# Sigmoid attention and an MLP mixer in one kernel: c1's first half loaded by unit, more dummy products at the start, opening cycles dealt anew, and two stores and two sums put off by a batch

## The chip, the cores and the metric

The kernel runs on one core of a Trainium2 chip. The metric is the device time of one execution in microseconds; the time before is the median of three runs. The profile is one more execution, taken with the hardware profiler on.

## What is computed

For each of 8 batches, attention with a sigmoid in place of the softmax runs over 12 heads of 448 tokens and 64 channels. Its output, with the heads joined to 768 channels, goes through a mixer: a two-layer network along the tokens, added to its input, and a two-layer network along the channels, added again.

```python
def _attn_ref(q, k, v):
    scores = scale * np.matmul(q, k.transpose(0, 1, 3, 2)) - np.log(S)
    attn = 1.0 / (1.0 + np.exp(-scores))
    return np.matmul(attn, v)
...
def _moe_ref(x, w_tok1, w_tok2, w_ch1, w_ch2):
    h = np.maximum(x.transpose(0, 2, 1) @ w_tok1, 0.0) @ w_tok2
    u = x + h.transpose(0, 2, 1)
    h2 = np.maximum(u @ w_ch1, 0.0) @ w_ch2
    return u + h2
```

w_tok1 is 448 x 256, w_tok2 256 x 448, w_ch1 768 x 1536, w_ch2 1536 x 768. The program calls them w1, w2, c1 and c2. The work is done in fp16 with fp32 sums.

## The kernel before

**Units and cycles.** A batch has three units of four heads, so there are 24 cycles (batch b, unit u). In each, `qk` (L182) is called for seven groups of tokens: four TensorE products of 64 rows and 64 columns each, which run side by side as a quad, and one ScalarE sigmoid over 128 x 896 (L194). The scores go through two PSUM buffers, so a score waits for the sigmoid two before it. `av` (L208) multiplies with v, and VectorE copies the sum to `xu`. The token network follows one to two cycles later (`tok_tail` L267, `tok1` L285, `ytrans` L312), on `xn`, a transpose of `xu`.

**Operands.** q and k come by DMA through GpSimd's queue with a cast to fp16 (`load` L113), are regrouped by VectorE (`relayout` L123, tiles `rel_k` and `rel_q`) and transposed by DMA on SyncE's queue (`dma_transpose` L141, tiles `tr_k` and `tr_q`); in the opening they are transposed on TensorE instead (`pe_transpose` L166). GpSimd also holds back later loads: `gated_loads` (L1125) copies two columns of a transposed tile, which waits for that tile, and the loads behind it in the queue start then. Weights are loaded in the same queue: `load_c1` (L974) and `load_c2` (L981) bring a half each, in an order written out by hand from L955 on.

**Opening** (L1038 to L1182). TensorE starts on dummy products (`keep_warm` L1026) until the first q is there. Then come three cycles of batch 0 with TensorE work put between the scores by a table, a stretch in which batch 1 begins and the first products of c1 are made (`ch1` L357, units in the order of `BY_UNIT`), and two cycles written out in a loop (L1139, cycles 4 and 5). There two blocks of c1 columns are made by `ch1_pair` (L396) in two turns: in turn 0 the upper rows of the array write one PSUM bank and the lower rows the other, in turn 1 they change places. The value products of the cycle before stand between the turns.

**Cycles 6 to 8** (from L1237) finish batch 0's c2 products by pieces (`work`), and cycle 8 ends with `sevens(1)`: c1 for batch 1 by a scheme with seven products instead of eight (`ch1_seven` L459), for which sums of weights are made beforehand. For c2 the like is done by `ch2_seven` (L763); its four sums of weights t1 to t4 are made on VectorE by `output_sums` (L735), twelve pieces of 128 x 768, into two tiles, hsum_a (t1, t2) and hsum_b (t3, t4). hsum_b lies in the same buffer as `out_first`, which holds batch 0's first two output tiles. Eight pieces are made during `sevens(1)`, one in cycle 9, three at the start of cycle 10.

**Steady cycles** (`steady` L1305) run from cycle 9 (batch 3, unit 0) on. While batch b is scored, batch b - 2 goes through c2. In unit 0 products 1 and 2 of the seven are made as a pair (`two_jobs` L854; between its turns `turn_over` L850, a copy of one column on VectorE, reads a bank), then 6 and 5 (`plain` L811, TensorE line L814); in unit 1 the pair 7 and 3 (TensorE line L861), then 4; in unit 2 the rest of the output. Products 1, 6, 7 and 4 add up in one bank, and VectorE adds each stand of it to the output (`end` L834, line L841) before the next one goes in. Regrouping pieces for the next batch are taken from a list, `within` and `behind` of them in a cycle.

**Stores.** `store` (L618) sends an output tile in two DMAs on SyncE's queue, 192 KB each, as soon as it is complete. This queue carries the DMA transposes too, `xtrans_dma` (L242), `dma_transpose` and `utrans` (L337, tile `un`), in program order.

Of the kernel before, what the change touches and what calls it, by code (L numbers as in the profile page):

```python
# [9 lines left out]
FP16 = mybir.dt.float16  # L10
# [11 lines left out]
NJ = 7  # L22
NP = 64
NU = 3
# [6 lines left out]
def kernel(  # L31
# [364 lines left out]
    def ch1_pair(b, cb):  # L396

        ps = [bank([128, 512], FP32, f"c1_{b}_{cb + p}") for p in range(2)]

        def step(turn, n):  # L400
            quads(
                ps,
                S,
                turn,
                lambda p, part, m: c1[
                    part, BY_UNIT[n], 128 * (cb + p) + m : 128 * (cb + p) + m + 64
                ],
                lambda p, part: ut(b, BY_UNIT[n])[part, 0:S],
                n == 0,
                n == NDB - 1,  # L410
            )

        def end():
            for p in range(2):
                ch1_out(b, cb + p, ps[p])

        turns = [[lambda t=t, n=n: step(t, n) for n in range(NDB)] for t in range(2)]
        return turns[0], turns[1], end
# [196 lines left out]
        if half == 1 and done:  # L615
            store(b, t)

    def store(b, t):  # L618
        for par in range(2):
            queue = nc.scalar if b == B - 1 and par == 1 else nc.sync  # L620
            queue.dma_start(
                out=orow[b, 2 * t + par],
                in_=outs[b, t][64 * par : 64 * par + 64, :],
            )
# [107 lines left out]
    LOW, HIGH = slice(0, NCB // 2), slice(NCB // 2, NCB)  # L732
    D1, D2 = slice(0, DH), slice(DH, D)

    def output_sums():  # L735

        for tag in ("hsum_a", "hsum_b"):
            pair = pa.tile([128, 2, NCB // 2, DH], FP16, tag=tag, bufs=1, name=tag)
            hsums.extend(pair[:, n, :, :] for n in range(2))
        t1, t2, t3, t4 = hsums  # L740

        def one(out, in0, in1, op):
            return [
                lambda k=k: nc.vector.tensor_tensor(
                    out=out[:, k : k + 2, :],
                    in0=in0[:, k : k + 2, :],
                    in1=in1[:, k : k + 2, :],
                    op=op,
                )
                for k in range(0, NCB // 2, 2)  # L750
            ]

        return [
            *one(t1, c2[:, LOW, D2], c2[:, LOW, D1], SUB),
            *one(t2, c2[:, HIGH, D2], t1, SUB),
            *one(t3, c2[:, HIGH, D2], c2[:, LOW, D2], SUB),
            *one(t4, c2[:, HIGH, D1], t2, SUB),
        ]
# [189 lines left out]
    nc.vector.memset(bias_t[:, :], att_bias)  # L948
    for b in range(2):
        nc.vector.memset(xu(b)[:, :, :, S:512], 0.0)  # L950
    nc.vector.memset(w1[64:128, 3, :], 0.0)
    load_first_k(2, NJ)
    load(0, "q", q, 1, 2)
    load(0, "k", k, 1, 2)
# [4 lines left out]
    for par in range(2):  # L959
# [2 lines left out]
            out=w1[part, 0:3, :],  # L962
            in_=tok_rows[0:6].rearrange("(t par) p c -> par p t c", par=2)[par],
        )
    nc.gpsimd.dma_start(out=w1[0:64, 3, :], in_=tok_rows[NJ - 1])
    load(0, "v", v, 1, 2)
    nc.gpsimd.dma_start(
        out=w2s[:, :, :], in_=moe_w_tok2.rearrange("(tc t) s -> t tc s", tc=2)
# [2 lines left out]
    load(1, "q", q, 0, 1)  # L971
    load(1, "k", k, 0, 1)

    def load_c1(half):  # L974
        cols = slice(CC // 2 * half, CC // 2 * half + CC // 2)
        nc.gpsimd.dma_start(
            out=c1[:, :, cols],
            in_=moe_w_ch1.rearrange("(db d) c -> d db c", db=NDB)[:, :, cols],
        )

    def load_c2(half):  # L981
# [3 lines left out]
            in_=moe_w_ch2.rearrange("(cb c) d -> c cb d", cb=NCB)[:, :, cols],  # L985
        )

    load(1, "q", q, 1, 2)
    load(1, "k", k, 1, 2)
    load_c1(0)  # L990
    load(1, "v", v, 0, 1)
    load(1, "q", q, 2, NU)
    load(1, "k", k, 2, NU)
# [1 line left out]
    load(1, "v", v, 1, NU)  # L995
    load(2, "q", q, 0, 1)
    load(2, "k", k, 0, 1)
    load_c2(0)
    load(2, "k", k, 1, NU)
    load(2, "q", q, 1, NU)  # L1000
    load_c2(1)
    load(2, "v", v, 0, 1)

# [32 lines left out]

    nc.scalar.activation(out=gate[:, 0:1], in_=bias_t[:, :], func=SIGMOID)
    heat[0] = bank([128, 512], FP32, "heat")  # L1038
    keep_warm(16)

    nc.vector.tensor_copy(out=raw_tile(0, "q")[:, 0, :, 0:4, :], in_=first_q[:, :, 0:4, :])
    nc.scalar.activation(
# [103 lines left out]
    for c, cb in ((N_FIRST, 3), (N_FIRST + 1, 8)):  # L1146
        b, u = divmod(c, NU)
        before = divmod(c - 1, NU)
        ahead = divmod(c + 1, NU)
        copies = []  # L1150

        def whole(cb):
            for d in range(0, NDB, 3):
                ch1(0, cb, d, d + 3)
                if copies:
                    copies.pop(0)()

        turn0, turn1, end = ch1_pair(0, cb)
        if c > N_FIRST:
            qk(b, u, 0)  # L1160
        qk(b, u, 1)
        for f in turn0:
            f()
        qk(b, u, 2)
        av(*before, 0, 4)
        qk(b, u, 3)
        av(*before, 4, NJ)
        if c - 1 in ON_DMA:
            xtrans_dma(*before)
        qk(b, u, 4)  # L1170
        for f in turn1[:4]:
            f()
        qk(b, u, 5)
        for f in turn1[4:]:
            f()
        end()
        qk(b, u, 6)
        if u == 2:
            copies = by_unit(2, 1)
        whole(cb + 2)  # L1180
        if c - 1 not in ON_DMA:
            xtrans(*before)  # L1182
        for t in ("k", "q"):
            pe_transpose(ahead[0], t, ahead[1])
        whole(cb + 3)
        if c == N_FIRST:
            tok1(*before)
            whole(cb + 4)
            nc.gpsimd.dma_start(out=w1[64:128, 3, :], in_=tok_rows[NJ - 1])
            ytrans(*before)  # L1190
        else:
            for w, f in pieces_ch2(0, by_half[:2]):
                f()
                if copies:
                    copies.pop(0)()
            while copies:
                copies.pop(0)()

            nc.gpsimd.tensor_copy(out=gate[:, :], in_=tr[2, "q"][:, 1, NJ - 1, 126:128])
            load(2, "v", v, 1, NU)  # L1200
            gated_loads(b)
# [19 lines left out]
    for c in range(2 * NU, ONE_RUN):  # L1221
        b, u = divmod(c, NU)
        before, ahead = divmod(c - 1, NU), divmod(c - 2, NU)


        if c == 2 * NU:
            first = c
            pending, shares = [*pieces_ch2(0, by_half[2:]), *pieces_last(0)], [10, 10, 10]
            total = sum(w for w, f in pending)
            spent = 0  # L1230

        def work(share):
            goal = 3 * sum(shares[: c - first]) + share * shares[c - first]
            done = 0
            while pending and spent + done < total * goal / 90:
                w, f = pending.pop(0)
                if len(pending) % 4 == 3:  # L1237
                    lane[0] ^= 1
                at_bank[0] = 2 + lane[0]
                f()  # L1240
                done += w
                if copies:
                    copies.pop(0)()
                elif early:
                    early.pop(0)()
            return done

        some(len(copies))
        qk(b, u, 0)
        qk(b, u, 1)  # L1250
        at_bank[0] = 0
        av(*before)
        xtrans_dma(*before)
        qk(b, u, 2)
        if c == 2 * NU + 2:
            copies += through_dma(3, 0)[NU + 1 :]
        spent += work(1)
        qk(b, u, 3)
        qk(b, u, 4)
        if u < 2:  # L1260
            at_bank[0] = 0
            tok_tail(*ahead)
            tok1(*ahead, with_scores=True)
        spent += work(2)
        if c == 2 * NU + 2:
            utrans(b - 1)
            token_sums(b - 1)
            spent += work(3)
        qk(b, u, 5)
        qk(b, u, 6)  # L1270
        at_bank[0] = 0
        if u < 2:
            ytrans(*ahead)
        else:
            tok_tail(*ahead)
            tok1(*ahead, with_scores=True)
        if c == 2 * NU + 1:
            copies += through_dma(3, 0)[: NU + 1]
        if u < 2:
            spent += work(3)  # L1280
        if u == 2:
            assert not copies
            extra = output_sums()
            copies += extra[:8]
            del extra[:8]
            sevens(b - 1)
            at_bank[0] = 0
            ytrans(*ahead)
            gated_loads(b)
    assert not copies and not pending and not early  # L1290

    def more(n):
        for f in extra[:n]:
            f()
        del extra[:n]
# [9 lines left out]
    def steady(b, u):  # L1305

        lot, before, ahead = b - 2, divmod(NU * b + u - 1, NU), divmod(NU * b + u - 2, NU)
        within, behind = ((0, 1), (3, 4), (0, 0))[u]

        def run(steps, n):  # L1310
            for f in steps[:n]:
# [4 lines left out]
        if u < 2:  # L1316
# [23 lines left out]
            if u == 0:  # L1340
                if b + 1 < B:
                    nc.gpsimd.tensor_copy(out=gate[:, :], in_=outs[lot, 0][:, 0:2])
                    load(b + 1, "q", q, 0, NU)
                seven.sums(2, 4)
                more(1)
            score()
            some(within)
            at_bank[0] = Y
            tok_tail(*ahead)
            tok1(*ahead, with_scores=True)  # L1350
# [2 lines left out]
        else:  # L1353
# [4 lines left out]
            score()  # L1358
            run(steps, 5)
            send = end(put_off=True)  # L1360
            score()
            at_bank[0] = Y
            av(*before, 0, 5)
# [23 lines left out]
        if u == 1:  # L1387
            utrans(b - 1)
        some(behind)
        if u == 1 and b < B - 1:  # L1390
            gated_loads(b)

    for c in range(ONE_RUN, N_CYCLES):
# [100 lines left out]
```

## Time and profile before

| what | us |
|---|---|
| median of three runs | 340.45 (340.07 to 340.86) |
| the profiled execution | 341.39 |
| its span, first to last instruction | 339.6 |
| TensorE products busy | 332.2 |
| VectorE busy | 234.9 |
| ScalarE busy | 213.0 |
| GpSimd's queue, share of the 16 DMA engines | 42.1% |
| SyncE's queue, share of the 16 DMA engines | 47.8% |

PE stands for TensorE's products, PEld for its weight loads, DVE for VectorE, ACT for ScalarE, POOL for GpSimd, SP for SyncE. A line such as L194 is the kernel's. In a timeline a row gives the start in the span, the time from the first start to the last end, engine, line, operation, tile written and tiles read, shape and count; in brackets stands the idle time of the engine before it and what ended it. In the chain of waits a row gives start, time on the chain, and who spent it. Ends of TensorE products are modelled, so a busy TensorE is not one at its peak: I compare the starts of neighbouring groups with the number of columns. In the list of DMA issues the last column is the time from issue to landing.

### The profile page before, as it was taken

The numbers are of one execution on the slowest core, as the hardware profiler recorded it, in microseconds if no ns is written. First come the engines' busy times: TensorE is split into PE (matmuls) and PEld (weight loads), VectorE is DVE, ScalarE is ACT, GpSimd is POOL, SyncE is SP. The second block draws the span as 40 slices with busy tenths as digits, with TensorE's granted clock in tenths as the row PEclk, the third lists the DMA queues.
The fourth block names the chain that finished last, engine by engine and source line by source line (L and its number), as shares of the span: only waits on it lengthen the run. The fifth ranks groups of instructions, "written<-read, shape, count | busy, mean of one in ns | idle before, by whom it ended". The sixth has DMA issues, their size and how long they took to land.

```text
span 339.6 us, 10285 instructions
## 1 busy us (share of the span) xinstructions
PE 332.2 (98%) x4423; PEld 242.5 (71%) x4423; DVE 234.9 (69%) x484; ACT 213.0 (63%) x272; POOL 58.7 (17%) x102
## 2 busy tenths in 40 slices
PE   7999999999999999999999999999999999999994
PEld 4555565555796679866896679866896679769852
DVE  2277366678998973877768773878758654876882
ACT  3997657388647895578647895578647795314200
POOL 8981550050031000220032002020010000000000
PEclk9999999999999999999999999999999999999999
DMA  7999999999999999998999899988995293028007
GB/s 119 173 174 195 206 205 204 163 175 237 169 187 189 140 168 211 185 142 161 204 145 172 138 206 175 206 117 134 196 175 93 56 193 73 2 56 185 4 11 197
DMA packets 104381, 52.17 MB, mean 154 GB/s; under 512 B 76432, under 2 KB 101264, under 8 KB 104336
## 3 DMA queue, kind: packets, MB, share of 16 engines
q1 hardware_dynamic: 78704, 29.11, 47.8%
q0 software_dynamic: 25168, 21.50, 42.1%
q10 hardware_dynamic: 464, 0.92, 1.0%
q8 instruction: 34, 0.56, 0.7%
q14 instruction: 11, 0.09, 0.1%
HBM read 43.45 MB, written 11.01 MB: 160 GB/s over the span
## 4 chain that ended last, share of the span: by engine, by line
PE 86%; DMA 5%; POOL 4%; ACT 2%; issue 1%; DVE 0%; ACTq 0%; POOLq 0%
PE c_ab L514 14%; PE c L814 10%; PE qk L187 9%; PE c_c L514 8%; PE xa L218 7%; PE c L861 6%; PE tk L296 5%; PE yt L316 5%; PE c L387 4%; DMA c<-in_moe_w_ch_dram 4%; PE c L584 4%; PE c L364 3%; PE c L669 3%; PE c L650 2%; ACT att L194 2%; DMA raw_v<-in_v_dram 2%
## 5 line engine op out<-in xcount | busy, mean ns | idle before, releaser
L194 ACT ACTIVATE att<-qk,att_bias 128x896 f16<-128x896 f32 x168 | 156.0, 1012 | 38.6 <-PE qk L187 37.6
L187 PE MATMUL qk<-tr_q,tr_k 64*64 64x448 f16 x672 | 61.3, 360 | 0.3 <-ACT att L194 0.2
L514 PEld LDWEIGHTS <-c 128*128 128x128 f16 x504 | 48.4, 98 | 1.1 <-issue 0.3
L218 PE MATMUL xa<-att,raw_v 64*64 64x448 f16 x644 | 40.7, 349 | 0.0
L187 PEld LDWEIGHTS <-tr_k 64*64 64x64 f16 x672 | 25.2, 105 | 19.0 <-issue 11.9
L514 PEld LDWEIGHTS <-sum 128*128 128x128 f16 x378 | 36.3, 98 | 0.0
L227 DVE CAST xu<-xa 128x448 f16<-128x448 f32 x40 | 23.1, 619 | 18.8 <-PE xa L218 18.4
L535 ACT ACTIVATE pt_ab<-c_ab 128x896 f32<-128x896 f32 x21 | 19.2, 917 | 20.6 <-PE c_ab L514 20.6
L218 PEld LDWEIGHTS <-raw_v 64*64 64x64 f16 x672 | 22.0, 107 | 8.3 <-issue 0.4
L861 PE MATMUL c<-c,h 64*64 64x384 f16 x360 | 24.6, 322 | 0.0
L1127 POOL COPY gate<-tr_q 128x2 f16<-128x2 f16 x6 | 1.6, 275 | 121.7 <-DMA tr_q<-rel_q 121.7
L326 DVE TENSOR_TENSOR xu<-xu,yt 128x448 f16<-128x448 f16 x38 | 21.7, 613 | 0.0
L537 ACT ACTIVATE h<-c_ab 128x896 f16<-128x896 f32 x7 | 6.4, 917 | 24.4 <-PE c_ab L514 24.4
L296 PE MATMUL tk<-xn,w 128*128 128x256 f16 x156 | 21.2, 274 | 0.1
L544 DVE TENSOR_TENSOR h<-pt_ab,c_ab 128x896 f16<-128x896 f32 x14 | 15.2, 1084 | 8.6 <-PE c_ab L514 8.6
L544 DVE TENSOR_TENSOR h<-pt_c,c_c 128x448 f16<-128x448 f32 x21 | 12.9, 614 | 11.7 <-PE c_c L514 11.6
L316 PE MATMUL yt<-w,h 128*128 128x448 f16 x88 | 20.3, 353 | 0.0
L841 DVE TENSOR_TENSOR o<-un,c 128x384 f32<-128x384 f16 x32 | 17.4, 550 | 4.0 <-PE c L814 4.0
L310 ACT ACTIVATE h<-tk 128x256 f16<-128x256 f32 x42 | 14.2, 406 | 9.5 <-PE tk L296 9.5
L814 PEld LDWEIGHTS <-hid 128*128 128x128 f16 x132 | 12.9, 98 | 8.0
L514 PE MATMUL c_ab<-diffs,c 128*128 128x224 f16 x168 | 18.4, 259 | 0.0
L296 PEld LDWEIGHTS <-w 128*128 128x128 f16 x156 | 13.6, 98 | 5.7 <-issue 2.4
(134 smaller groups left out, 572.1 us busy)
## 6 DMA issues: line engine op xcount, KB each, us to landing
out_dram<-o SPq DMA_DIRECT2D x41, 192.0 KB, 3.2
c<-in_moe_w_ch_dram POOLq DMA_DIRECT2D x4, 1152.0 KB, 16.1
raw_k<-in_k_dram POOLq DMA_DIRECT2D x10, 336.0 KB, 6.9
raw_q<-in_q_dram POOLq DMA_DIRECT2D x10, 336.0 KB, 5.7
raw_v<-in_v_dram POOLq DMA_DIRECT2D x10, 336.0 KB, 8.8
out_dram<-o SPq DMA_DIRECT2D x15, 96.0 KB, 2.4
raw_q<-in_q_dram POOLq DMA_DIRECT2D x12, 112.0 KB, 5.1
raw_k<-in_k_dram POOLq DMA_DIRECT2D x12, 112.0 KB, 5.4
```

The lines of the kernel that those rows point to most:

```text
L187: nc.tensor.matmul(out=ps[64 * g : 64 * g + 64, hi, 0:S], lhsT=tr[b, "k"][64 * hi : 64 * hi + 64, u, j, 64 * g : 64 * g + 64], rhs=tr[b, " ...
L194: nc.scalar.activation(out=att[b, u, j][:, :, :], in_=ps[:, :, 0:S], func=SIGMOID, bias=bias_t[:, :], scale=att_scale,)
L218: nc.tensor.matmul(out=ps[g][64 * hi : 64 * hi + 64, 0:S], lhsT=raw[b, "v"][64 * g : 64 * g + 64, u, hi, j, :], rhs=att[b, u, j][64 * g : ...
L227: nc.vector.tensor_copy(out=xu(b)[:, u, g, 0:S], in_=ps[g][:, 0:S])
L296: nc.tensor.matmul(out=ps[tcb], lhsT=w1[rows, t, cols], rhs=xn[b, u][rows, :, t, :], start=(t == 0 and not with_scores), stop=(t == (2 if ...
L316: nc.tensor.matmul(out=ps[:, 0:S], lhsT=h1[b, u][:, tcb, g, :], rhs=w2[:, tcb, :, :], start=(tcb == 0), stop=(tcb == 1),)
L326: nc.vector.tensor_tensor(out=x, in0=x, in1=ps[:, 0:S], op=ADD)
L514: nc.tensor.matmul(out=ps[:, g, p, :], lhsT=weights[n][:, d, 128 * cb : 128 * cb + 128], rhs=moving[n][:, d, :], start=(n in (1, 5, 2) and ...
L535: nc.scalar.activation(out=shaped(part[:, :, :]), in_=ps, func=COPYF)
L544: nc.vector.tensor_tensor(out=shaped(dst), in0=shaped(parts[gs, which]), in1=ps, op=ADD)
L814: nc.tensor.matmul(out=ps[:, 0:DH], lhsT=self.weights[n][:, k, :], rhs=self.moving[n][:, k, :], start=(n in (1, 2, 5) and k == 0), stop=(k ...
L861: nc.tensor.matmul(out=ps[m : m + 64, 0:DH], lhsT=lhsT(n)[part, m : m + 64], rhs=rhs(n)[part, :], start=(opens and turn == 0 and n == 0), ...
```

## The change

- c1's first half comes as three transfers, one for each unit's two blocks of rows; the first goes ahead of q and k of batch 1, unit 1. c2's first half goes behind q and k of batch 2, unit 1.
- w1's last 64 rows are loaded into both halves of the tile at the start; a memset and a later load of the second half go.
- 21 dummy products stand at the start instead of 16.
- In cycles 4 and 5 the scores are spread otherwise: turn 0 of `ch1_pair` is split by a score, a `turn_over` follows it, and cycle 5's first score moves into cycle 4.
- The four stores of batch 0's output tiles 0 and 1 are kept in a list and issued at the end of cycle 8.
- `output_sums` is called by half. t1 and t2 are made in cycle 8; t3 and t4, for which hsum_b is taken only after those stores are issued, in cycle 9 (three pieces) and cycle 10 (three).
- The regrouping pieces of batch 4 move from (0 and 1, 3 and 4, 0 and 0) to (0 and 0, 4 and 2, 2 and 0), and that batch's `gated_loads` from cycle 10 to cycle 11.

```diff
     def ch1_pair(b, cb):
         ps = [bank([128, 512], FP32, f"c1_{b}_{cb + p}") for p in range(2)]
+        turn_bank[0] = ps[1]
...
+    later = []
+
+    def store(b, t, put_off=True):
+        if b == 0 and t < 2 and put_off:
+            later.append(t)
+            return
...
-    def load_c1(half):
+    def load_c1(half, u=None):
         cols = slice(CC // 2 * half, CC // 2 * half + CC // 2)
+        blocks = slice(0, NDB) if u is None else slice(u, NDB, NU)
...
+    load_c1(0, 0)
     load(1, "q", q, 1, 2)
     load(1, "k", k, 1, 2)
-    load_c1(0)
+    load_c1(0, 1)
+    load_c1(0, 2)
...
+    load(2, "k", k, 1, 2)
+    load(2, "q", q, 1, 2)
     load_c2(0)
-    load(2, "k", k, 1, NU)
-    load(2, "q", q, 1, NU)
+    load(2, "k", k, 2, NU)
+    load(2, "q", q, 2, NU)
...
-    keep_warm(16)
+    keep_warm(21)
...
         turn0, turn1, end = ch1_pair(0, cb)
-        if c > N_FIRST:
-            qk(b, u, 0)
         qk(b, u, 1)
-        for f in turn0:
+        for f in turn0[:3]:
             f()
         qk(b, u, 2)
+        for f in turn0[3:]:
+            f()
+        turn_over(turn_bank[0])
+        qk(b, u, 3)
         av(*before, 0, 4)
-        qk(b, u, 3)
+        qk(b, u, 4)
         av(*before, 4, NJ)
...
             tok1(*before)
+            qk(*ahead, 0)
             whole(cb + 4)
-            nc.gpsimd.dma_start(out=w1[64:128, 3, :], in_=tok_rows[NJ - 1])
...
-            extra = output_sums()
-            copies += extra[:8]
-            del extra[:8]
+            copies += output_sums(0)
             sevens(b - 1)
             at_bank[0] = 0
             ytrans(*ahead)
+            for t in later:
+                store(0, t, put_off=False)
+            extra = output_sums(1)
             gated_loads(b)
...
-        within, behind = ((0, 1), (3, 4), (0, 0))[u]
+        within, behind = (
+            ((0, 0), (4, 2), (2, 0)) if b == NU else ((0, 1), (3, 4), (0, 0))
+        )[u]
...
                 seven.sums(2, 4)
-                more(1)
             score()
             some(within)
+            if u == 0:
+                more(3)
```

## Prediction

> **What bounds the kernel now.** I read the page first, then the chain of waits in order of time, then the timelines of TensorE (PE), ScalarE (ACT), VectorE (DVE) and SyncE (SP), and the list of DMA issues with their times to landing. From the page and the chain:
>
> ```profile
> PE 332.2 (98%) x4423; PEld 242.5 (71%) x4423; DVE 234.9 (69%) x484; ACT 213.0 (63%) x272; POOL 58.7 (17%) x102
> ```
> ```profile
> 21.01 12.64 DMA c<-in_moe_w_ch_dram
> ...
> 101.28 0.76 PE yt L316 x4
> ...
> 139.59 0.76 PE yt L316 x4
> ```
>
> The first column is the start, the second the time on the chain. The reader is to see that PE is busy throughout, that a load of c1 ends a wait at 33.65 us, and that a steady batch lasts 38.31 us (139.59 - 101.28; the next begins at 177.90): after 33.7 nearly every step of the chain is PE's, so there is little to win there, only to lose. What can go lies before 60 us. The timelines of the opening, PE and the one ACT row:
>
> ```profile
> 1.05 3.59 PE L1028 MATMUL heat<-warm 128*128 128x256 f16 x16 [1.05 <-DVE att_bias L948]
> 5.83 0.96 PE L170 MATMUL tp_q<-ident,raw_q 128*64 128x128 f16 x14 [1.18 <-DVE raw_q L1041]
> ...
> 11.34 0.58 PE L170 MATMUL tp_q<-ident,raw_q 128*64 128x128 f16 x14
> ...
> 32.54 1.03 PE L296 MATMUL tk<-xn,w 128*128 128x256 f16 x8
> 33.70 0.93 PE L364 MATMUL c<-xu_first,c 128*128 128x448 f16 x4
> ...
> 44.42 0.38 PE L187 MATMUL qk<-tr_q,tr_k 64*64 64x448 f16 x4 [0.16 <-ACT att L194]
> ```
> ```profile
> 10.61 19.58 ACT L194 ACTIVATE att<-qk,att_bias 128x896 f16<-128x896 f32 x21 [0.38 <-PE qk L187]
> ```
>
> Three things: fourteen transposes cost 0.96 us at 5.83 and 0.58 at 11.34, so PE's clock is low at first; from 10.61 to 30.2 sigmoids follow each other without a gap, 0.93 us apart, so ACT paces that stretch; at 33.70 c1's first product waits for c1.
>
> **The change, part by part.** The sum is made in the time of the profiled execution (341.39 us, of which 339.6 are its span); that one lies 0.94 above the median of the runs, 340.45, and I add the sum to the median.
>
> *21 dummies.* Sixteen take 3.59 us, 0.21 apart. Five more are 1.07 us and fit in the 1.18 us in which PE waits for raw_q: no cost. PE's pace changes within the score group at 10.01 us, 4.5 us after that pause ended. With the pause filled PE works unbroken from 1.05, so I expect the fast pace at about 5.6. Then the transposes at 5.83 take 0.58, ACT's copy of tr_q ends 0.38 earlier, three dummies take 0.50 instead of 0.82, the first scores start at 7.05 instead of 7.68, and the first sigmoid at 7.5 instead of 8.33. The gap of 0.38 us before 10.61 goes too, since the ten transposes and the copy of tr_k finish by 8.5: the third sigmoid comes at 7.5 + 2 x 0.93 = 9.4 instead of 10.61. **-1.2 us**; bounds 0 (the pace does not move) and -1.25. The whole ACT-paced stretch shifts with it; the operands allow that, the tightest being q and k of batch 1, unit 1 (below). The Trainium skill, "TensorE: Matmul & The Clock Gate", Part 1, says that the clock rises after one busy window of about 3.4 us whose phase is not tied to the kernel's start; by that rule the rise would come anywhere from 4.5 to 7.9 us, and the sum would vary by some 0.6 us between executions. No run here shows its phase yet.
>
> *c1's first half by unit.* The eight token products at 32.54 take 0.87 us where nothing waits (48.64 in the chain), so of the 1.16 us up to 33.70 some 0.29 is the wait for c1, which landed at 33.65 (issued 21.01). As three transfers, the first goes ahead of q and k of (1, 1), the second ends a third of c1's stretch earlier: k of (1, 1) landed at 25.9, so (33.65 - 25.9) / 3 = 2.6 us earlier, 31.1, plus 0.2 for the extra 32 KB of w1. PE asks at 33.41 - 1.2 = 32.2. The third unit, 33.85, is asked for at about 36.6; q and k of (1, 1), now 28.5, at 31.48 - 1.2 = 30.3. All covered: **-0.29**; bounds 0 and -0.29.
>
> *Opening cycles.* In cycle 4 PE waits 0.50 us for ACT before the score at 44.42 (0.87 us from 43.55 to 44.42 for eight products worth 0.37), in cycle 5 0.39. With turn 0 split, the sixth score still needs the fourth sigmoid, 0.49 + 3 x 0.93 + 1.01 = 4.3 us after the first score starts, and PE has 22 quads of 0.187 = 4.1 us to do in between: about 0.2 us is left in each cycle. The score moved ahead of `whole(cb + 4)` stands among 128-row products, and going to the small tiles and back costs 0.11 each way (66.14 to 66.44 for 0.19 of work). The `turn_over` copy is 0.15 us on DVE with 1.3 us of value products behind it. 0.89 - 0.4 - 0.23: **-0.26**; bounds -0.6 and +0.3. These three parts make -1.75, and below PE is 1.7 us ahead.
>
> *Loads.* DMA is nine tenths busy from 4 to 66 us, so a transfer moves only by the bytes put ahead of it. c2's first half has 448 KB more ahead: 53.6 + 2.3 = 55.9, asked for at 60.09 - 1.7 = 58.4. The thinnest cover is xn of (1, 1): issued 56.30, landed 66.4, read at 68.40 - 1.7 = 66.7. I take 0, with +0.5 in the range.
>
> *Stores put off.* Four stores of 192 KB leave SP at 77.6 to 80.3 and stand behind un and the o_3 stores instead. SP then issues without a pause (start, time to issue):
>
> ```profile
> 82.98 4.00 SPq L142 DMA_TRANSPOSE tr_k<-rel_k  x1
> ...
> 89.76 4.47 SPq L142 DMA_TRANSPOSE tr_q<-rel_q  x1
> 94.33 3.73 SPq L343 DMA_TRANSPOSE un<-xu  x1
> 98.15 1.18 SPq L923 DMA_DIRECT2D out_dram<-o  x2
> ```
>
> *c2's last sums.* All six t3 and t4 pieces now need hsum_b, which shares its buffer with out_first, so the first of them waits on DVE for all four stores. The first three stand here on DVE:
>
> ```profile
> 108.55 0.55 DVE L744 TENSOR_TENSOR hsum_b<-c 128x768 f16<-128x768 f16 x1
> 109.01 1.05 DVE L841 TENSOR_TENSOR o<-un,c 128x384 f32<-128x384 f16 x2
> 109.98 1.14 DVE L326 TENSOR_TENSOR xu<-xu,yt 128x448 f16<-128x448 f16 x2
> ```
>
> Two things follow. First, three pieces stand there instead of one (two came from the sevenfold stage, where no PE wait goes with them): +0.94 us (1.49 - 0.55). The two L841 that follow free the banks in which PE's next products accumulate; they ended at 110.06 and PE's L861 began at 110.56. So 0.94 - 0.5 = 0.45 of PE wait, 0.1 more at the value products (the L326 ends late), 0.1 at the last split, since three copies of rel_k now precede that bank's release: **+0.7**; bounds +0.4 and +1.0. Cycles 10 and 11 hide the rest: DVE waited 1.6 us before 122.97.
>
> Second, the wait itself. DVE asks at 108.55 - 1.7 = 106.85. SP's chain starts 1.7 earlier, and its first transpose is no longer behind stores: 3.28 (128.85) instead of 4.00. So tr_q lands 2.5 earlier than at 96.05, and the gate lets the loads of v and k go 2.5 earlier than 96.69. Those four landed at 103.9, 105.9, 108.1 and 109.7; the two o_3 stores, issued at 98.15 and 98.79, at 103.4 and 105.4: one store to each load. Of the issues from 98.75 to 98.90 the last column is the time to landing:
>
> ```profile
> raw_k<-in_k_dram POOLq DMA_DIRECT2D x1, 336.0 KB, 11.1
> out_dram<-o SPq DMA_DIRECT2D x1, 96.0 KB, 6.6
> ```
>
> If that goes on, the four stores share the turns of the loads of k (now 105.6 and 107.2, plus 0.5 for the store's own bytes) and two come behind: 107.7 + 2 x 0.5 = 108.7. **+1.8 us** on DVE and one for one on PE, since DVE had no idle time left and PE's L861 waits behind it. Bounds: 0, if the stores land 6.0 us after issue as the last did at 80.3 (99.3 + 6.0 = 105.3), and +2.7, if SP gains only the 1.7. I take 1.8: the o_3 stores are the nearest row, the same queue at the same loads.
>
> Sum: -1.2 - 0.29 - 0.26 + 0.7 + 1.8 = **+0.75**: 341.2 us (342.1 in a profiled execution like this one).
>
> **Rivals.** *The stores are there in time.* DVE does not wait: 340.45 - 1.75 + 0.7 = 339.4, faster. For it: stores without loads beside them land 2.3 to 6 us after issue. It decides at a landing of 106.85 us. Against it: stores issued amid loads at 173.83, 135.46 and 211.37 took 5.3 to 6.0 each, and the last of four has three ahead of it.
>
> *Two stores to a load.* At 210.78 and 211.37 two stores landed at 215.7 and 217.4, both before the second load at 219.3. Then the four end with the second load of k, 107.7: a wait of 0.85, and 340.45 - 1.75 + 0.7 + 0.85 = 340.25, no change. The Trainium skill, "DMA: Bandwidth & Descriptors", Queues, rings and completion order, says that each DMA engine takes turns between queues by packets of some 9 to 17 descriptors; by that rule a load would be more than one packet and this rival would hold; the o_3 rows agree less with it than the pair at 210.78.
>
> *The pace of PE does not move*, as the window may need more than the filled gap: 341.2 + 1.2 = 342.4.
>
> The built order has separate waits for c1's three units at L364, so that part does what it says.
>
> **How the numbers follow.** Chances: forecast 0.45, stores in time 0.27, two to a load 0.18, pace unmoved 0.10. The range reaches from the second case less the spread of the opening's terms (339.2) to the last (342.8). A measurement of this kernel can tell about 0.2% (0.68 us) from no change. Faster: nearly all of stores in time and a little of two to a load, 0.28. Slower: most of the forecast, all of the last, 0.47. Within: 0.25.
>
> **What would show it.** The fast pace near 5.6 us and the first sigmoid near 7.5; no DMA wait at the first c1 product, which starts near 32.2; in cycle 9 on DVE an idle time before the first hsum_b piece, put down to the out_first stores, and an idle time of PE before L861 in cycle 10 that is about 0.5 longer. A steady batch stays 38.31 us. Wrong would be: no idle time before hsum_b (stores in time), or PE waiting at xn in cycle 6, or a sigmoid train that starts where it did.

## The result, and the profile after

The changed kernel takes 344.34 us (median of six runs, 341.55 to 346.15), the kernel before beside it 340.65. The ratio is 1.0095, 95% interval 1.0067 to 1.0124: 3.2 us slower. The forecast was 0.75 slower, 341.2, with a range up to 342.8; the sign was right, the size far too small.

The profiled execution took 343.17 us. First the page's busy times and its chain of waits in order of time (start, time on the chain, who spent it):

```profile
PE 332.7 (97%) x4428; PEld 243.7 (71%) x4428; DVE 234.5 (69%) x485; ACT 213.1 (62%) x272; POOL 62.1 (18%) x108
```
```profile
54.87 12.55 DMA xn<-xu
...
74.81 12.41 DMA raw_q<-in_q_dram
...
101.38 8.17 DMA out_dram<-out_first
...
141.21 0.76 PE yt L316 x4
...
179.52 0.76 PE yt L316 x4
```

TensorE has the same work, and a steady batch is still 38.31 us (179.52 - 141.21). But three transfers stand on the chain between 54 and 110 us where before there was TensorE: xn of unit (1,1), raw_q of batch 3, and the stores that were put off. The opening, timelines of PE and ACT:

```profile
5.80 0.64 PE L170 MATMUL tp_q<-ident,raw_q 128*64 128x128 f16 x14
...
31.18 1.03 PE L296 MATMUL tk<-xn,w 128*128 128x256 f16 x8
32.05 0.92 PE L364 MATMUL c<-xu_first,c 128*128 128x448 f16 x4
```
```profile
7.46 21.37 ACT L194 ACTIVATE att<-qk,att_bias 128x896 f16<-128x896 f32 x23 [0.48 <-PE qk L187]
```

The transposes at 5.80 take 0.64 instead of 0.96, the sigmoids start at 7.46 instead of 8.33 and run without a gap, and c1's first product follows the token products by 0.87 us, so it no longer waits. Then DVE, where the lead goes:

```profile
87.24 0.62 DVE L129 COPY rel_q<-raw_q 128x896 f16<-128x896 f16 x1 [2.18 <-DMA raw_q<-in_q_dram]
...
109.67 1.49 DVE L750 TENSOR_TENSOR hsum_b<-c 128x768 f16<-128x768 f16 x3 [0.77 <-DMA out_dram<-out_first]
```

In brackets stand the waits: 2.18 us for raw_q, 0.77 us for the stores. In the profile before, the same copy had no wait:

```profile
84.76 0.62 DVE L129 COPY rel_q<-raw_q 128x896 f16<-128x896 f16 x1
```

Not all of such a wait reaches TensorE: in the second profile of the changed kernel DVE waited 1.76 us for raw_q, and TensorE lost 0.14 us between 48 and 101.

How far TensorE is ahead (-) or behind (+) of the shown profile of before is read at three places: the token product that starts at 48.48 there, and the last ytrans group (L316) of cycle 8 (101.12) and of cycle 11 (139.43). From the last of them to TensorE's last product, seventeen of the twenty traces run alike to 0.05 us, the others up to 0.34 us longer; what follows that product varies by 0.3 us. With further profiles of the two kernels, taken in the experiments:

| execution | time | at 48 | at 101 | at 139 |
|---|---|---|---|---|
| before, as shown | 341.39 | 0 | 0 | 0 |
| before, second | 341.48 | -0.62 | -0.06 | -0.05 |
| before, third | 340.94 | -0.45 | -0.45 | -0.45 |
| changed | 343.17 | -1.85 | +0.27 | +1.62 |
| changed, second | 341.43 | -1.91 | -1.77 | 0.00 |
| changed, third | 341.27 | -1.79 | -1.85 | -0.24 |
| changed, fourth | 346.37 | -1.74 | -0.08 | +4.95 |

The middle step (48 to 101) is the loads, the last (101 to 139) holds the put-off stores and the late sums. Both differ from execution to execution, and that is the scatter of the times.

### The profile page after: what moved, and what is told of

Its sections match the earlier page's. It is cut to its first block, busy times and chain, and to the rows that moved or that the text cites. A ratio compares the mean times of both kernels' runs of the same rounds, so it can differ in the third digit from the quotient of the medians.

```text
span 341.4 us, 10299 instructions
## 1 busy us (share of the span) xinstructions
PE 332.7 (97%) x4428; PEld 243.7 (71%) x4428; DVE 234.5 (69%) x485; ACT 213.1 (62%) x272; POOL 62.1 (18%) x108
## 4 chain that ended last, share of the span: by engine, by line
PE 77%; DMA 11%; DVE 5%; ACT 3%; issue 1%; SPq 1%; POOL 1%; DVEq 0%
PE c_ab L516 12%; PE c L825 10%; PE qk L187 8%; PE c_c L516 8%; PE xa L218 7%; PE c L872 5%; PE tk L296 5%; PE c L387 5%; PE yt L316 4%; DMA xn<-xu 4%; DMA raw_q<-in_q_dram 4%; ACT att L194 3%; PE c L676 3%; DMA out_dram<-out_first 2%; PE c L657 2%; PE c L364 2%
## 5 line engine op out<-in xcount | busy, mean ns | idle before, releaser
L218 PEld LDWEIGHTS <-raw_v 64*64 64x64 f16 x672 | 23.0, 107 | 8.1 <-issue 0.4
L316 PE MATMUL yt<-w,h 128*128 128x448 f16 x88 | 20.3, 353 | 0.0
L872 PEld LDWEIGHTS <-h 64*64 64x64 f16 x360 | 14.4, 107 | 4.6 <-issue 0.4
```

The source lines that it names most:

```text
L218: nc.tensor.matmul(out=ps[g][64 * hi : 64 * hi + 64, 0:S], lhsT=raw[b, "v"][64 * g : 64 * g + 64, u, hi, j, :], rhs=att[b, u, j][64 * g : ...
L316: nc.tensor.matmul(out=ps[:, 0:S], lhsT=h1[b, u][:, tcb, g, :], rhs=w2[:, tcb, :, :], start=(tcb == 0), stop=(tcb == 1),)
L872: nc.tensor.matmul(out=ps[m : m + 64, 0:DH], lhsT=lhsT(n)[part, m : m + 64], rhs=rhs(n)[part, :], start=(opens and turn == 0 and n == 0), ...
```

## Experiments

Theory S: the stores and late sums make the loss. Theory L: the loads, which the forecast had at 0, give the opening's lead back.

**1. The two halves of the change.** The first kernel takes the put-off stores and late sums out of the change, the second puts them alone into the kernel before. The moved regrouping pieces and the moved `gated_loads` of batch 4 go with them both times, so what is called stores and sums below includes these.

```diff
-    def store(b, t, put_off=True):      # first kernel; second: the reverse
+    def store(b, t):
...
-            copies += output_sums(0)
+            extra = output_sums()
```

> Opening edits alone (dummies, w1 in two transfers, c1 by unit, cycles 4 and 5 dealt anew, order of the loads around c2); the stores of batch 0 and the sums of c2 stay as in the kernel before. If the loads cost nothing, as the prediction had it, the lead of 1.75 us stays: about 338.9. If the loads give the lead back, as the trace of the changed kernel reads (1.0 at the value of tk in cycle 6, 0.24 at the scores of 86.6, 0.95 in the sevenfold stage), it is 340.65 - 1.9 + 2.2 = about 341.0, with PE waiting for xn near 67 and VectorE waiting over 1 us for raw_q near 87.

> The other half alone: stores of batch 0's two tiles put off, t3 and t4 dealt to cycles 9 and 10, the opening and the loads as in the kernel before. By the prediction's terms +0.7 + 1.8 = 2.5: about 343.1, with VectorE waiting 1.8 us for out_first. By what the trace of the changed kernel lost between 101 and 141 us (1.62 - 0.27) it is +1.35: about 342.0; VectorE, no longer late, would wait longer than the 0.77 us it waits there. If the stores are no cost of their own, 340.65 to 341.2.

Opening alone: 342.64 against 341.13, ratio 1.0055 (1.0032 to 1.0077). Stores alone: 342.80, 1.0048 (1.0026 to 1.0070). So each half loses some 1.6 to 1.9 us, and both theories hold, for a half each; the 341.0 expected of the first by theory L was too low. In the profile of the opening alone the lead of 1.68 us at 48 became +0.97 at 101 and +2.21 at 139; DVE shows both steps:

```profile
86.99 0.62 DVE L129 COPY rel_q<-raw_q 128x896 f16<-128x896 f16 x1 [2.54 <-DMA raw_q<-in_q_dram]
...
113.36 0.62 DVE L129 COPY rel_k<-raw_k 128x896 f16<-128x896 f16 x1 [1.19 <-issue]
```

The second wait is a load too: raw_k of batch 4 landed at 113.28. With the stores alone the step from 101 to 139 was 1.73, with 1.16 us of DVE's wait in front of hsum_b.

**2. The whole change with one thing undone.** First the order of the loads around c2, then the delay of the stores.

```diff
-    load(2, "k", k, 1, 2)               # first kernel
-    load(2, "q", q, 1, 2)
     load_c2(0)
-    load(2, "k", k, 2, NU)
-    load(2, "q", q, 2, NU)
+    load(2, "k", k, 1, NU)
+    load(2, "q", q, 1, NU)
...
-        if b == 0 and t < 2 and put_off:   # second kernel
-            later.append(t)
-            return
```

> The changed kernel with the loads around c2 in the old order (c2's first half ahead of the rest of k and q of batch 2, which go as one transfer each again). If the order around c2 makes the losses between 66 and 101 us, they go: 344.3 - 2.2 = about 342.1. If the number of small transfers ahead (c1 in three pieces, w1 in two) makes them, most stays: 343.5 to 344.3, with PE still waiting for xn near 67. If the stores make the whole loss, 344.3.

> The changed kernel with the four stores issued at once as before; the sums t3 and t4 still stand in cycles 9 and 10. If the wait for the stores costs what the trace shows, VectorE's 0.77 us before hsum_b goes and the time falls by 0.8 to 1.2, to 343.1 to 343.5. If put-off stores are free, 344.3. If the stores when early take turns from the transposes near 82 us, as in the kernel before, the sevenfold stage starts no earlier and the gain is below 0.5.

Old order: 342.55, ratio 1.0047 (1.0023 to 1.0071), 1.6 us below the whole change, with some 1.1 us of uncertainty in such a difference of two ratios. Its profile keeps 1.59 of lead up to 101 and loses 1.88 to the stores: Theory L for the first stage, S for the second, in one trace. Stores at once: 344.92, 1.0123 (1.0090 to 1.0156), no gain where 0.8 to 1.2 us was expected, although its profile (340.48) had no wait for the stores and lost only 0.49 from 101 to 139. This contradiction stayed open until experiment 6.

**3. What in the opening is worth something.** The opening edits with the old loads; with the new order but k and q merged into pieces of 224 KB, all ahead of c2; and the 21 dummies alone.

```diff
-    load(2, "k", k, 1, 2)               # second kernel
-    load(2, "q", q, 1, 2)
+    load(2, "k", k, 1, NU)
+    load(2, "q", q, 1, NU)
     load_c2(0)
-    load(2, "k", k, 2, NU)
-    load(2, "q", q, 2, NU)
...
-    keep_warm(16)                       # third kernel, all of it
+    keep_warm(21)
```

> Opening edits with the old order and sizes of the loads around c2 (c2's first half ahead of the rest of k and q of batch 2, one transfer each); stores and sums as before. If the new order is what gives the lead back, all of it stays: 341.1 - 1.6 = about 339.5, no thinning of the DMA rate at 46 to 49 us, no wait for xn near 67. If c1 in three pieces and w1 in two are enough to make the loads late, it is 341 to 342.6 like the opening with the new order (342.64).

> Opening edits with the new order, but the rest of k and of q of batch 2 go as one transfer of 224 KB each, both ahead of c2's first half: two transfers fewer, and 224 KB more ahead of c2 than in the changed kernel. If the loss comes from many small transfers (GpSimd issues one only when the one eight earlier has landed, so 0.9 MB is all that is in flight), the rate at 46 to 49 us stays above 190 KB per us, c2's second half lands near 64.5 and the time is about 339.5. If it comes from what stands ahead of c2, it is no better than 342.6.

> The kernel before with 21 dummies in place of 16, and nothing else. By the prediction's term, full pace near 5.6 us and 1.2 less: about 339.9. If an earlier start of the score train only means earlier waits for loads, the time is that of before, 341.1, with TensorE waiting for c1 1.2 longer near 33 us. If the pace of TensorE does not move, full pace near 10.4 us and 341.1.

341.45, 341.50 and 341.00 beside 341.20: ratios 0.9997 (0.9975 to 1.0019), 1.0009 (0.9986 to 1.0032) and 1.0000 (0.9977 to 1.0023). None comes to the 339.5 to 339.9 that was expected of a lead that stays. Two things follow. The new order, with its smaller pieces, costs the opening 1.6 to 2.0 us (1.0055 against 1.0009 and 0.9997), and the bytes ahead of c2 are not the reason, for the merged kernel has more of them. (Each call for k or q sends two DMAs, one for each half of the partitions, so merging makes it four DMAs fewer and puts 448 KB more ahead of c2, not two and 224 as expected above.) GpSimd's queue, timeline of the changed kernel, and the windows (length, busy times by engine, clock, DMA share, GB/s) of the kernel before, the changed and the merged kernel:

```profile
35.59 1.82 POOL L118 DMA_DIRECT2D raw_k<-in_k_dram  x3
42.03 0.60 POOL L118 DMA_DIRECT2D raw_k<-in_k_dram  x1 [4.62 <-DMA c<-in_moe_w_ch_dram]
43.17 0.59 POOL L118 DMA_DIRECT2D raw_q<-in_q_dram  x1 [0.54 <-DMA raw_v<-in_v_dram]
44.26 0.59 POOL L118 DMA_DIRECT2D raw_q<-in_q_dram  x1 [0.50 <-DMA raw_v<-in_v_dram]
44.84 1.04 POOL L997 DMA_DIRECT2D c<-in_moe_w_ch_dram  x1
```
```profile
46.00:49.00 3.00, 3.00 (x48) 2.21 (x46) 2.60 (x5) 0.17 (x1) 2.83 (x4) 1.00 1.31 206
```
```profile
46.00:49.00 3.00, 3.00 (x23) 1.69 (x21) 1.15 (x2) 1.30 (x3) 3.00 (x5) 1.00 1.05 153
```
```profile
46.00:49.00 3.00, 3.00 (x23) 1.70 (x22) 1.40 (x3) 1.04 (x3) 1.61 (x3) 1.00 1.27 207
```

The load at 42.03 goes out when c1's second column half, issued eight loads earlier at 30.59, has landed (41.75), the next when the one after that has. This limit is the program's: in the trace's records GpSimd's loads take eight semaphores in turn, and a load waits for its own semaphore, which the load eight earlier raises. So the big transfer of c2 is issued 7 us later than before (44.84 for 37.58), and the seven loads then in flight ahead of it have 112 KB each, 784 KB in all or some 4 us at 200 GB/s. From 46 to 49 us the rate falls to 153 GB/s, and the DMA share from 1.31 to 1.05. In the merged kernel c2 is issued late too, at 44.35, but the seven ahead of it hold 1232 KB, and the rate is 207, as before (206). The shortfall is (207 - 153) x 3 = 162 KB, 0.8 us of transfer. How this becomes 1.6 to 2.0 us in the medians is not traced: of the ten profiles with the new order five lost nothing between 48 and 101 us (-0.06 to 0.16) and five lost 1.66 to 3.82; of the three with the old order or merged loads and no further edit at the loads, none lost more than 0.74.

Second, the lead itself hardly shows in the medians. The merged kernel's profiled execution kept its 1.65 us to the end (339.88); the old-order one lost 0.74 at raw_q of batch 3 (landed at 85.48) and 1.02 at raw_k of batch 4, and 0.66 already at 23.5 us at raw_q of (1,0). A lead of TensorE moves none of the loads of the first 50 us, which are issued from the start and keep their pace.

**4. Does the lead make the loads later?** In the profile before, xn of unit (2,0) is issued at 76.25, 2.66 us behind raw_q of batch 3, and raw_q lands 8.90 us after its issue. With the lead xn follows raw_q by 0.1 to 2.2 us, and raw_q takes 10.7 to 13.6 us. (Without the opening edits xn follows by 2.7 to 3.1 us, and three of the four profiles show 8.7 to 8.9 us, the fourth 12.0.) The edit holds that transpose back until raw_q is there (old-order kernel):

```diff
+        if c == 2 * NU + 1:
+            late = pc.tile([128, 2], FP16, name="late")
+            nc.sync.dma_start(out=late[:, :], in_=raw[3, "q"][:, NU - 1, 1, NJ - 1, E - 2 : E])
         xtrans_dma(*before)
```

> The opening edits with the old order of loads, and one edit more: ahead of the transpose xn of unit (2,0), SyncE sends a DMA of 512 bytes that reads the end of raw_q of batch 3, so that this transpose is issued only when that load has landed (near 82) and not at 74.6 to 75 beside it. If the earlier TensorE spoils its own gain by starting this transpose amid the loads of k and q (their rate falls from 200 to about 140 KB per us and raw_q lands at 83 to 87 in place of 82.5), raw_q lands by 82.5, VectorE's rel_q does not wait, the sevenfold stage starts on time and the time is about 339.5 to 340. If raw_q is late for another reason, 341.4 as without the edit, or more, since SyncE's stores wait too.

346.50, ratio 1.0158 (1.0125 to 1.0191): much slower, but not where theory L was tested. raw_q, issued at 73.68, landed at 83.32 instead of 84.75 (second profile of the changed kernel, issued at 73.62), DVE did not wait, and TensorE lost nothing between 48 and 101 us. The same kernel without the edit had issued it at 73.37, and it landed at 85.48. From 78.5 to 80.5 us GpSimd's queue moved 0.41 MB with the transpose held back; in that profile of the changed kernel it moved 0.29 MB, beside 0.09 MB of SyncE's. So in these executions the traffic beside the loads takes 1.4 to 2.5 us of raw_q's time. The price came later: SyncE, held up to 83.4, was late with everything behind, the loads of batch 4 followed, and DVE waited 4.55 us for raw_k at 115.9. The other way, xn of (2,0) on TensorE (merged kernel):

```diff
-        xtrans_dma(*before)
+        if c != 2 * NU + 1:
+            xtrans_dma(*before)
...
+        if c == 2 * NU + 1:
+            at_bank[0] = 0
+            xtrans(*before)
```

> The opening with merged loads (as in the run of that name, 341.5), and unit (2,0)'s xn made on TensorE (eight transposes and one copy on VectorE, about 0.5 us of TensorE) instead of by the DMA transpose that SyncE issues near 74.6 amid the loads of batch 3. If that transpose is what makes raw_q late, the loads keep some 200 KB per us from 78 to 81 us, raw_q of batch 3 lands at 80.5 to 82 (83.0 before this edit, up to 87 with the new order), and no execution loses time in the sevenfold stage: about 340.5, less scatter. If raw_q is late for another reason, it lands at 83 to 85 as without the edit and the time is 341.5 to 342.

341.69, ratio 1.0024 (1.0006 to 1.0043), with little scatter (341.27 to 342.52). raw_q landed at 82.93, no earlier than in the merged kernel (83.02): the out_first stores, issued at 74.95, now ran beside it instead. From 78.5 to 80.5 us SyncE's queue moved 0.38 MB and GpSimd's 0.19 MB. TensorE lost 1.67 us to the eight transposes and to a wait for xn. So it is not this transpose alone that slows the load: SyncE's stores do it too.

**5. Further profiles of the two kernels.**

> The kernel before, unchanged, for a second profile; its shown one took 341.39 us where the median is 341.1. If the gain of the 21 dummies is missing because the pace of TensorE often rises early without them, this execution has its full pace well before 10 us and its first token product well before 20.0. If it is missing because the loads take it back, the pace rises at 9 to 11 us again, and raw_q of batch 3 lands near 82 without a transpose beside it.

> The same once more, as a third draw of where the pace of TensorE rises in the kernel before: 9 to 11 us by the two openings with 16 dummies that have been seen, 4.2 to 6.8 us if these were exceptions.

> The changed kernel, unchanged, for a second profile. By the reading so far it has the thinner DMA rate at 46 to 49 us, the wait for raw_q between 84 and 88 us and the wait of VectorE for out_first before hsum_b; if one of the three is missing, it was a chance of the first profile.

> The changed kernel a third time. Its runs lie between 341.4 and 346.2; one profile had no loss at the loads (341.43), one 2.2 us (343.17). If the slow ones lose at the loads, an execution above 344 shows over 3 us of waits for xn, raw_q and raw_k between 66 and 116 us and steady batches of 38.31. If they lose elsewhere, the steady batches or the opening up to 66 us are longer.

> The changed kernel a fourth time, for the same question as the third: where an execution above 344 loses its time. By either reading the wait of VectorE for out_first stays, 0.7 to 1.4 us.

The kernel before: with 16 dummies the first token product came at 20.07, 19.75 and 19.44 (19.86 with the stores alone); the pace rose at 9.3 to 10.4 us each time. In sixteen executions with 21 dummies the product came at 18.62 to 19.25, on average 18.84, and the pace rose at 3.7 to 7.0 us. So the dummies are worth 0.9 us at that product, not the 1.2 read from the latest of four draws. The Trainium skill, "TensorE: Matmul & The Clock Gate", Part 1, says that the window in which the clock is judged runs freely and does not start with the kernel; these traces agree, with rises spread over 3.2 us behind the same 21 products. Raw_q of batch 3 landed at 84.68 and 81.79 in the second and third profile of the kernel before; the second, with TensorE 0.62 us ahead, gave back all but 0.06.

The changed kernel: the second profile had all three signs, a rate of some 150 GB/s near 47 us, DVE's wait for raw_q and that for out_first. The stage of the stores cost 1.77 and 1.61 in the second and third profile, as with the stores alone. DVE of the second:

```profile
108.04 1.50 DVE L750 TENSOR_TENSOR hsum_b<-c 128x768 f16<-128x768 f16 x3 [1.18 <-DMA out_dram<-out_first]
```

It asked at 106.86; the stores landed at 105.70 to 107.92, the first just ahead of the second load of v (105.87), the others between it and the first of k (108.68): all four landed around one load, and not one to a load. In the fourth the loads were late (raw_q at 86.86), the last store landed at 111.20, DVE waited 2.77 us, more than the 0.7 to 1.4 expected, and TensorE 2.67. Timeline of PE and windows:

```profile
113.34 0.35 PE L872 MATMUL c<-hsum_b,hid 64*64 64x384 f16 x2 [2.67 <-DVE o L852]
...
115.25 2.07 PE L218 MATMUL xa<-att,raw_v 64*64 64x448 f16 x16
```
```profile
112.00:114.00 2.00, 0.55 (x10) 0.28 (x13) 2.00 (x5) 0.44 (x1) 0.00 (x0) 1.00 1.59 133
114.00:116.00 2.00, 2.00 (x40) 1.36 (x35) 2.00 (x5) 0.14 (x1) 0.00 (x0) 0.72 1.35 155
116.00:118.00 2.00, 2.00 (x28) 1.31 (x24) 0.29 (x2) 1.14 (x2) 0.00 (x0) 0.50 1.48 157
118.00:120.00 2.00, 2.00 (x44) 1.36 (x36) 1.72 (x4) 1.69 (x3) 0.00 (x0) 0.92 0.35 52
```

The granted clock, the column before the DMA share, falls to 0.72, 0.50 and 0.92: (0.56 + 1.0 + 0.16) / 0.5 = 3.4 us at half pace. The next group starts at 116.74, so sixteen value products worth 0.75 us take 1.49. With TensorE busy throughout, that is 1.7 us on top of the wait; the stage cost 5.03.

**6. Why issuing the stores at once gained nothing.** The second kernel of experiment 2 again.

> The changed kernel with the four stores issued at once, looked at once more, for a second profile: its first had 340.48 us and its median was 344.92. If the loss is a matter of loads that land just in time or too late, this execution loses 1 to 4 us between 66 and 116 us at waits for xn, raw_q or raw_k, and the steady batches of 38.31 us are the same to 0.02. If the time is lost elsewhere, a steady batch or the end is longer.

> The changed kernel with the four stores issued at once, a third time (340.48 and 342.4 in its two profiles, median 344.92). The stores are no wait here by either reading; an execution above 344 must show its loss at the loads (xn near 67, raw_q at 84 to 88, raw_k near 112) if these are the cause of the scatter.

> The changed kernel with the four stores issued at once, a fourth look: its profiles took 340.48, 342.4 and 340.43 us, its median in five rounds was 344.92. A slow execution of the changed kernel (346.37) lost 2.9 us at the wait for out_first and 2.0 more to a halved clock of TensorE right behind it. If an execution of this kernel above 344 shows a granted clock of 0.5 behind some wait of over 2 us, its scatter has the same second step with another wait in front (raw_q or raw_k); if its clock is full, its scatter has another cause.

> The same kernel, a fifth look for the same question. An execution near 340.5 shows waits below 2 us and a full clock throughout.

Its five profiles, with the loss from 48 to 101 and from 101 to 139 us:

| time | 48 to 101 | 101 to 139 |
|---|---|---|
| 340.48 | -0.06 | 0.49 |
| 342.40 | 2.00 | 0.63 |
| 340.43 | -0.05 | 0.50 |
| 345.52 | 0.16 | 5.01 |
| 344.60 | 3.82 | 0.57 |

In four of the five the last stage costs 0.5 to 0.6, the price of the late sums and of the pieces moved with them, so the wait for the stores is 1.0 to 1.3 of the 1.6 to 1.8. The rest is the loads. The 344.60 lost 3.82 us there, at a full clock (the expectation named an execution near 340.5, and this was none); rows of PE and DVE:

```profile
67.66 0.30 PE L277 MATMUL tk<-xn,w 64*64 64x256 f16 x4 [0.65 <-DMA xn<-xu]
88.45 0.30 PE L277 MATMUL tk<-xn,w 64*64 64x256 f16 x4 [0.95 <-DMA xn<-xu]
```
```profile
84.49 1.67 DVE L129 COPY rel_k<-raw_k 128x896 f16<-128x896 f16 x3 [3.66 <-issue]
89.27 0.62 DVE L129 COPY rel_q<-raw_q 128x896 f16<-128x896 f16 x1 [1.81 <-DMA raw_q<-in_q_dram]
```

The 345.52 waited for xn, issued at 105.61 and landed at 117.03, while the rate fell to 44 GB/s, and the clock fell again:

```profile
117.07 0.43 PE L277 MATMUL tk<-xn,w 64*64 64x256 f16 x4 [2.56 <-DMA xn<-xu]
```
```profile
114.00:116.00 2.00, 0.51 (x10) 0.10 (x2) 1.97 (x6) 1.67 (x2) 0.00 (x0) 1.00 1.55 44
116.00:118.00 2.00, 0.93 (x7) 0.57 (x8) 0.96 (x2) 0.00 (x0) 0.00 (x0) 0.69 1.51 181
118.00:120.00 2.00, 2.00 (x10) 1.09 (x8) 0.00 (x0) 0.77 (x2) 0.00 (x0) 0.50 1.35 147
```

So the contradiction is one of draws: the gain of 1.0 to 1.3 us is there in the last stage of every profile without a late transfer in that stage, and a median over six executions that scatter by 7 us does not show it. Why the DMA engines come to 44 GB/s in such a stretch stays open; no run isolates it.

## Why the prediction was wrong, step by step

**21 dummies, -1.2.** Mechanism right (pace near 6 us in the profiled execution, sigmoids at 7.46 for a forecast 7.5), size 0.9, since the profile of before was the latest of four draws of the rise. For the 4.5 to 7.9 us that the prediction works out for the rise, and its 0.6 us of variation, the traces have 3.7 to 7.0 us, and 0.63 us at the first token product.

**c1 by unit, -0.29.** Right: no wait, 32.05 for a forecast 32.2. **Opening cycles, -0.26.** About right: the profiles gain 0.2 between 35 and 48 us.

**"Loads. ... I take 0."** This step failed, and with the most weight. It counted bytes, and by that count c2's first half came as said (56.27 for a forecast 55.9); but the program lets only eight of GpSimd's loads be in flight, and with the four small loads of k and q put ahead of c2 the eight held too few bytes to keep the rate from 46 to 49 us (153 for 207 GB/s). The order cost 1.6 to 2.0 us by the medians (1.0055 against 0.9997 and 1.0009; 1.0095 against 1.0047). That the order and size of these loads cost this is shown; how the 0.8 us of missing transfer grows to it is not. The cover named as thinnest, xn of (1,1), was thin indeed (landed at 67.42 for a forecast 66.4; 0.79 us idle before it), but raw_q of batch 3, not named, had the longer wait, 2.18 us on DVE.

**The lead of 1.7 "below".** The forecast carried it unchanged to 106.85 and to the end. The opening edits with the old loads are worth -0.1 in the median (0.9997, interval -0.85 to +0.65 us). This step failed too. Ahead by 1.7 us TensorE or DVE can meet a load that was in time before: raw_q of (1,0) in the old-order profile, and raw_k of batch 4, which in the profile before landed at 109.68 and was copied at 111.04. Raw_q of batch 3 is another case. In the profile before it landed at 82.49, which DVE, asking at 83.0 with the lead, would still have met; but SyncE's traffic, issued earlier with the lead, slows it by 1.4 to 2.5 us (experiment 4). Not every execution loses: the merged kernel's profile kept its 1.65 us.

**c2's last sums, +0.7.** 0.5 to 0.6. **The wait for the stores, +1.8.** The wait is there, at the place forecast, but too large in the sum: in the second profile, which still had its lead, DVE asked at 106.86 (forecast 106.85; in the shown one, its lead gone, at 108.90), the last store landed at 107.92 (108.7) and the wait was 1.18, between the forecast and the rival with two stores to a load. Neither rule of turns held, since all four landed around one load. Together the two terms are 1.4 to 1.7 by the medians (1.0095 against 1.0055, 1.0047 against 0.9997, 1.0048 alone), for a forecast 2.5. But the upper bound of +2.7, "one for one on PE", is no bound: in the one profile of the changed kernel where TensorE waited 2.67 us, the halved clock added 1.7.

By the medians then: -0.1 for the opening, +1.6 to +2.0 for the order of the loads, +1.4 to +1.7 for stores and sums; measured 3.2, each figure uncertain by about 1 us. The two errors, the loads and the lead that could not be kept, went the same way; the stores, taken too dear, hid 0.8 to 1.1 us of them. So the sign came right although the sum had a gain of 1.75 that the medians do not show and nothing for the loads. The upper end of the range is named as the last rival's time, which its sum gives as 342.4 and not 342.8.

## What to carry to other kernels

Before moving an engine forward, look at what it will ask for next: a transfer that has no wait in the profile may be in time only because the engine is late, and transfers that are issued earlier with the engine can slow a load that was in time. Where a program allows a fixed number of loads in flight, count the loads as well as their bytes, and keep a large one among the small so that the DMA engines have work while the next load waits to be issued. Price a wait on the busiest engine not only by its length but by what a longer one triggers, and take two or three profiles before a figure is read from a random phase.

## What was not expected of the hardware

An idle time of TensorE of 1.0 to 1.4 us left its clock at full, one of 2.67, 2.56 or 4.59 us halved it. The half pace lasted 3.4 us in the first two, 6.8 in the third, and began from 1.2 us before the end of the wait to 1.5 us behind it. The Trainium skill, "TensorE: Matmul & The Clock Gate", "Why this matters for your kernels", advises against idle gaps of over some 3 us; these runs show that 2.6 can be enough, while the length of 3.4 us agrees with the window of Part 1.

The clock records of the twenty traces show when a gap is enough. Each stretch at one pace between two changes is a whole multiple of 3.413 us (327.68, 331.09 and 334.51 us are 96, 97 and 98 of them), so the pace changes only at the ends of such windows. Laid over TensorE's rows, it fell behind the three windows with 1.97, 2.24 and 3.36 us of idle time and behind none with 1.40 or less; it rose behind windows with 0.74 us or less and behind none with 0.77 or more. This is also what the 21 dummies do: with 16, the window with the pause before raw_q had 0.77 to 1.23 us idle in all four executions, and the rise came one window later.

One kernel's executions differ by up to 5 us through the landing of transfers and the clock behind a long wait, with the same instructions in the same order.
